# Linear attention and MLP on one core: batch 0's output products in half banks, copied and summed by ScalarE, and the sums over exponentials moved

## The chip, the core and the metric

The kernel runs on one core of a Trainium2 chip. The core has a matrix engine (TensorE, PE in the profile; PEld is its weight load), a vector engine (VectorE, DVE), an activation engine (ScalarE, ACT), GpSimd (POOL) and SyncE (SP). Each works through its own queue of instructions in order, and semaphores tie them together. DMAs are issued from the queues of SP, ACT and POOL. The metric is device time in microseconds (us); lower is better.

## The reference

q, k and v are 8 batches x 8 heads x 576 positions x 64, float32. Per head, with softmax over the 64 features for q and over the 576 positions for k:

```python
kv  = einsum('bhsd,bhse->bhde', softmax(k, axis=2), v)       # 64 x 64 per head
att = einsum('bhsd,bhde->bhse', softmax(q, axis=-1), kv)
x   = att.transpose(0, 2, 1, 3).reshape(8, 576, 512)
xn  = (x - mean(x)) / sqrt(var(x) + 1e-6) * g
out = x + relu(xn @ w1) @ w2                                 # w1 512 x 2048, w2 2048 x 512
```

## The kernel before

Of each batch the first 512 positions are handled as four tiles (t = 0 to 3) of 128 positions; the last 64 positions of all eight batches together form a ninth "batch", C9. (For batch 0 the k and v of all 576 positions are taken at once, two heads on 128 partitions.) The factor 1 / standard deviation is left out of xn and multiplied into the output at the end (`rstds`), so that the MLP need not wait for it.

All five engines are scheduled by hand: the order in which the program calls operations is the order in each engine's queue. `run` (L830) takes a list of main steps, the matmuls of one batch's MLP, each with a weight, and a list of side steps (position, function). A side step is called before the first main step that starts at or after its position. Positions are so a count of matmul work: one step of 512 columns weighs 1, one of 256 columns 0.5. Main steps of batch c carry the preparation of batch c + 1 and the loads and exponentials of batch c + 2 as side steps.

For batches from the third on (c = 2 to 8, `mm1_fast` L747 and `mm2_fast` L677), the products are made in blocks of 2 x 2 with seven products instead of eight, from sums of blocks that DVE and GpSimd make (`sum_w1` L221, `quarter_w2` L559, `sum_x` L236, `sum_h` L572). The first product takes positions 0 to 56, in two groups of 28: in each group ACT copies (L768, L772), then DVE adds into a bank (`add_5` L774, instruction L775), then product 7 runs in the bank that this add read, DVE writes hT (L778, L783) and PE goes on. The second product takes positions 56 to 112; at its end DVE writes quarters of the output (`y_quarter` L605, instruction L610), four pairs, which free the PSUM banks. DVE also makes the products x = po / sum (L421), centres them (L407) and sums the exponentials of q over features (`reduce_q` L208, L210); `recip_q` (L858) inverts the sums.

Batch 0 is special (`first_batch` L943). Its MLP starts as soon as its first tile is ready, and w1 arrives only then: the POOL queue issues, behind a small copy (`gate`, L995) that waits for the first half of q, the loads of v, the second half of q, w1 in five pieces (two of 256 columns, three of 512), w2, and then q, k and v of the next batches. PE does warming matmuls on zeros (`warm` L844) in between. exp(k) is spread by DVE (L282) and ACT (L278) into block-diagonal tiles of 128 x 128 (two heads each), cleared first by a memset (L988); the sums z and the products kv are then 36 full matmuls each (L289, L301). The output product po of a tile is one bank of 512 columns (L370). For tile 0 DVE makes mean and variance with bn_stats and bn_aggr (L384, L385), for tile 1 ACT sums the mean (L434); xn = (x - mean) * g, with g broadcast over partitions by a matmul of g's row (L1022). PE transposes xn, ACT copies the transposes out (`pe_T` L914).

The main steps of batch 0 are `mm1_part` (L499, weights 0 to 64; parts of four m, each 128 of the 2048 columns, times one or two tiles t) and `mm2_stream` (L548, 64 to 128). Beside them (L1103 to L1136) stand the rest of batch 0's tiles, the scaling of w1 by g (`scale_w1` L212, for later batches) and batch 1's preparation: exponentials of q (L193), `reduce_q`, transposes, `sum_w1`, the cast of v by DVE (`cast_v` L132, L134), the exponentials of k's last 64 positions (L179), `kv_mm` (L319, L333), `kv_out`, and then po, x, xn and the transposes of batch 1's tiles, before batch 1's first product at 128. The change goes through `first_batch`, this list, `prep_fast`, `attn_fast`, `second_side` and `attn_rest`.

Of the kernel before, what the change touches and what calls it, by code (L numbers as in the profile page):

```python
# [20 lines left out]
def kernel(  # L21
# [51 lines left out]
    gate = const.tile([P, 4], FP32)  # L73
# [4 lines left out]
    ones_f = const.tile([1, P], FP32)  # L78
    g_bc = const.tile([P, DM], FP32)
# [190 lines left out]
    def exp_k0(j):  # L270

        if j == 0:
            eks[0] = raw.tile([P, NP, T0, D], BF16, tag="kt", name="ek0", bufs=1)
        if j < NP - 1:
            nc.scalar.activation(eks[0][:, j], raws[0][0][:, j], AF.Exp)
            return
        for ps in halves:
            nc.scalar.activation(raws["ek"][ps, j, :, ps], raws[0][0][ps, j], AF.Exp)  # L278

    def spread_k0(j):  # L280
        for ps in halves:
            nc.vector.tensor_copy(out=raws["ek"][ps, j, :, ps], in_=eks[0][ps, j])  # L282

    def z0_mm(j):

        if j == 0:
            kvbox["z0"] = mm_ps.tile([P, DM], FP32, tag="m", name="z0")
        for t in range(T0):
            nc.tensor.matmul(  # L289
                kvbox["z0"][:, j : j + 1], raws["ek"][:, j, t], ones,  # L290
                start=(t == 0), stop=(t == T0 - 1),
            )

    def kv0_mm(j):

        if j != 1:
            pool, tag = (mm_ps, "m") if j == 3 else (att_ps, "a")
            kvbox["p0"] = pool.tile([P, 2, 256], FP32, tag=tag, name="pkv")
        pkv = kvbox["p0"]
        for t in range(T0):  # L300
            nc.tensor.matmul(  # L301
                pkv[:, j % 2, 0:D], raws["ek"][:, j, t], raws["v0"][:, j, t],
                start=(t == 0), stop=(t == T0 - 1),
            )
        if j:
            js = slice(0 if j == 1 else j, j + 1)
            rz = kvbox["rz"]
            for half, ps in enumerate(halves):
                if half and j > 1:
                    nc.scalar.activation(  # L310
                        kv_sb[ps, 0, j, ps], pkv[ps, j % 2, 0:D], AF.Copy, scale=rz[ps, j : j + 1]
                    )
                else:
                    nc.vector.tensor_mul(
                        kv_sb[ps, 0, js, ps], pkv[ps, slice(0, 2) if j == 1 else slice(j % 2, j % 2 + 1), 0:D],
                        rz[ps, js].to_broadcast([64, js.stop - js.start, D]),
                    )
# [64 lines left out]
    def stats(c, t, src, parts=(slice(0, 512),)):  # L382
        x, st, xn, mv = xs[c]
        nc.vector.bn_stats(st[:, t], src)  # L384
        nc.vector.bn_aggr(mv[:, t], st[:, t])  # L385
        for cols in parts:
            nc.vector.scalar_tensor_tensor(
                xn[:, t, cols], in0=src[:, cols], scalar=mv[:, t, 0:1], in1=g_bc[:, cols],
                op0=ALU.subtract, op1=ALU.mult,
            )  # L390

    def square_sum(c, t):
        x, _, _, mv = xs[c]
        if c:
            nc.scalar.activation(  # L395
                scrap, x[:, t], AF.Square, bias=mv[:, t, 0:1], scale=-float(DM),
                accum_out=mv[:, t, 1:2],
            )
        else:
            nc.scalar.activation(  # L400
                scrap, x[:, t], AF.Square, bias=mv[:, t, 0:1], accum_out=mv[:, t, 1:2]
            )

    def xn_out(c, t):
# [3 lines left out]
            out=xn[:, t], in0=x[:, t], scalar1=float(DM), scalar2=mv[:, t, 0:1],  # L408
            op0=ALU.mult, op1=ALU.subtract,
        )  # L410

    def xn_first(t):
        x, _, xn, mv = xs[0]
        nc.vector.scalar_tensor_tensor(
            xn[:, t], in0=x[:, t], scalar=mv[:, t, 0:1], in1=g_bc, op0=ALU.add, op1=ALU.mult
        )

    def x_fast(c, t):

        x, st, _, mv = xs[c]  # L420
# [4 lines left out]
            accum_out=mv[:, t, 0:1] if c else st[:, t, 0:1],  # L425
        )
        if c:
            xn_out(c, t)
        else:
            nc.vector.tensor_scalar_mul(out=mv[:, t, 0:1], in0=st[:, t, 0:1], scalar1=-1.0 / DM)  # L430
            xn_first(t)

    def mean_x(c, t):
        nc.scalar.activation(  # L434
            scrap, pobox[c, t], AF.Copy, scale=-1.0 / DM, accum_out=xs[c][3][:, t, 0:1]
        )

    def xn_sub(c, t):
        _, _, xn, mv = xs[c]
        nc.vector.scalar_tensor_tensor(  # L440
            xn[:, t], in0=pobox[c, t], scalar=mv[:, t, 0:1], in1=g_bc, op0=ALU.add, op1=ALU.mult
        )

    def square_po(c, t):
        mv = xs[c][3]
        nc.scalar.activation(
            scrap, pobox[c, t], AF.Square, bias=mv[:, t, 0:1], scale=1.0, accum_out=mv[:, t, 1:2]
        )

    def x_out(c, t):  # L450

        x = xs[c][0]
        if c == 1 or (c == 0 and t < 2):
            stats(c, t, pobox[c, t])
            return
        if c < B:
            nc.vector.tensor_mul(
# [730 lines left out]
```

## Time and profile before

| | us |
|---|---|
| median of three runs (268.95 to 269.48) | 269.26 |
| the profiled execution | 268.44 |
| its span, first to last instruction | 266.6 |
| PE busy | 259.1 (97%) |
| DVE busy | 220.2 (83%) |
| ACT busy | 178.6 (67%) |
| POOL busy | 90.6 (34%) |
| granted TensorE clock, mean | 0.999 |

The profiled execution is one more run; 1.8 us of its time lie outside the span. Times inside a view count from the start of the span. A timeline row gives start, duration, engine, source line, operation, what is written from what (buffer numbers left out) and the shape, how often, and in brackets the idle time before it with what ended it. In a DMA row the last number is the time from issue to landing.

### The profile page before, as it was taken

Reading aid. Unit: us, or ns where it says so; the run is one execution under the profiler, and the core shown is the slowest. Engines: PE = TensorE matmul, PEld = TensorE weight load, DVE = VectorE, ACT = ScalarE, POOL = GpSimd, SP = SyncE. Lnnn points to the kernel's source line nnn. Section 1 sums busy time; section 2 is a strip of 40 time slices with the busy share of each in tenths; the row PEclk is TensorE's granted clock in tenths of the full one; section 3 lists DMA queues with packets and bytes.
Section 4 is the critical chain, followed back from the end, with each engine's and each line's share of the span. In section 5 each row is a group of like instructions: output and inputs, shape, how many; then the busy total and the mean of one; then the engine's idle time right before and its main releaser. Section 6 shows DMA issues by size and latency. Waiting matters only on the chain. (4 is left out here: it accounts for less than half of the span.)

```text
span 266.6 us, 6696 instructions
## 1 busy us (share of the span) xinstructions
PE 259.1 (97%) x2634; PEld 218.4 (82%) x2634; DVE 220.2 (83%) x471; ACT 178.6 (67%) x349; POOL 90.6 (34%) x145
## 2 busy tenths in 40 slices
PE   8999999999999999999999999999999999999993
PEld 5778855775988998899889988998989788888882
DVE  7974995878999899789988988998799968877872
ACT  4767881796966886688668866786686378438400
POOL 6933126213069104930781088109100800030000
PEclk9999999999999999999999999999999999999999
DMA  6999999979966998899589948996935130422014
GB/s 216 220 203 207 325 223 303 278 171 279 176 131 195 303 111 133 246 288 117 92 265 267 127 87 278 257 138 126 261 60 101 42 119 4 79 81 79 2 39 118
DMA packets 82329, 45.00 MB, mean 169 GB/s; under 512 B 58037, under 2 KB 78521, under 8 KB 82298
## 3 DMA queue, kind: packets, MB, share of 16 engines
q0 software_dynamic: 32800, 22.29, 44.9%
q1 hardware_dynamic: 48906, 21.77, 37.6%
q10 hardware_dynamic: 592, 0.52, 0.6%
q8 instruction: 20, 0.33, 0.5%
q14 instruction: 11, 0.09, 0.1%
HBM read 36.70 MB, written 9.44 MB: 173 GB/s over the span
## 5 line engine op out<-in xcount | busy, mean ns | idle before, releaser
L599 PEld LDWEIGHTS <-hs 128*128 128x128 bf16 x512 | 49.5, 98 | 5.7
L744 PEld LDWEIGHTS <-w_q 128*128 128x128 bf16 x448 | 43.0, 98 | 6.8 <-issue 1.0
L248 POOL TENSOR_TENSOR tq<-xnT 128x256 bf16<-128x256 bf16 x24 | 15.6, 665 | 77.2 <-DMA xnT<-xn 63.9
L599 PEld LDWEIGHTS <-hT 128*128 128x128 bf16 x384 | 37.1, 98 | 4.4
L744 PEld LDWEIGHTS <-w1g 128*128 128x128 bf16 x336 | 32.2, 98 | 3.9
L599 PE MATMUL ba<-w_q,hs 128*128 128x256 bf16 x256 | 31.7, 273 | 0.0
L775 DVE TENSOR_TENSOR bb<-bx,s 128x512 f32<-128x512 f32 x28 | 18.3, 695 | 14.1 <-ACT s L772 14.0
L744 PE MATMUL bx<-tq,w_q 128*128 128x256 bf16 x224 | 29.2, 273 | 0.1
L768 ACT COPY bc<-bx 128x512 f32<-128x512 f32 x28 | 15.2, 594 | 16.8 <-PE bx L744 16.8
L421 DVE SCALAR_TENSOR_TENSOR x<-po,rq 128x512 bf16<-128x512 f32 x34 | 23.3, 686 | 2.2 <-PE po L370 2.0
L395 ACT ACTIVATE scrap<-x,mv 128x512 bf16<-128x512 bf16 x32 | 23.0, 720 | 1.7 <-DVE x L421 1.3
L616 POOL DMA_DIRECT2D out_dram<-ot x28 | 15.4, 558 | 24.1 <-DVE ot L610 24.0
L786 ACT ACTIVATE hT<-bc 128x512 bf16<-128x512 f32 x28 | 15.5, 598 | 11.7 <-PE bc L744 11.7
L583 DVE TENSOR_TENSOR hs<-hT 128x1024 bf16<-128x1024 bf16 x32 | 21.7, 685 | 1.3 <-ACT hT L786 1.2
L370 PE MATMUL po<-kv_sb,eqT 128*128 128x128 bf16 x128 | 21.2, 219 | 0.0
L210 DVE TENSOR_REDUCE zq<-eq 128x16 f32<-128x1024 bf16 (+1 forms) x20 | 20.6, 1048 | 0.5 <-ACT eq L193 0.5
L778 DVE TENSOR_TENSOR hT<-bx,s 128x512 bf16<-128x512 f32 x28 | 18.0, 686 | 3.2 <-PE bx L744 3.2
L786 ACT ACTIVATE hT<-bb 128x512 bf16<-128x512 f32 x28 | 15.3, 600 | 8.1 <-PE bb L744 8.1
L624 ACT COPY s<-ba 128x512 f32<-128x512 f32 x15 | 8.7, 579 | 13.4 <-PE ba L599 8.7
L599 PE MATMUL ba<-w_sb,hT 128*128 128x256 bf16 x128 | 16.7, 273 | 0.0
L599 PE MATMUL bb<-w_q,hs 128*128 128x256 bf16 x128 | 16.6, 273 | 0.0
L772 ACT COPY s<-bb 128x512 f32<-128x512 f32 x28 | 15.8, 620 | 0.7 <-PE bb L744 0.7
(152 smaller groups left out, 555.1 us busy)
## 6 DMA issues: line engine op xcount, KB each, us to landing
out_dram<-ot POOLq DMA_DIRECT2D x32, 256.0 KB, 6.2
qt<-in_q_dram SPq DMA_DIRECT2D x5, 1024.0 KB, 6.8
kt<-in_k_dram SPq DMA_DIRECT2D x5, 1024.0 KB, 13.4
w_sb<-in_moe_w_ch_dram POOLq DMA_DIRECT2D x4, 512.0 KB, 16.5
qt<-in_q_dram POOLq DMA_DIRECT2D x2, 1024.0 KB, 14.6
kt<-in_k_dram POOLq DMA_DIRECT2D x2, 1024.0 KB, 15.2
vm<-in_v_dram POOLq DMA_DIRECT2D x16, 128.0 KB, 13.0
w_raw<-in_moe_w_ch_dram POOLq DMA_DIRECT2D x3, 512.0 KB, 12.3
```

The costliest lines, as they stand in the source:

```text
L210: nc.vector.reduce_sum(eqs[c][1][:, ts], eqs[c][0][:, ts], axis=AX.X)
L248: eng.tensor_tensor(out=dst[:, t], in0=x[:, t], in1=y[:, t], op=ALU.subtract)
L370: nc.tensor.matmul(pobox["p"][:, i * P : i * P + P], eqTs[c][:, t, i, :], kv_sb[:, c, i, :], start=True, stop=True,)
L395: nc.scalar.activation(scrap, x[:, t], AF.Square, bias=mv[:, t, 0:1], scale=-float(DM), accum_out=mv[:, t, 1:2],)
L421: nc.vector.scalar_tensor_tensor(x[:, t].rearrange("p (h d) -> p h d", h=H), in0=pobox[c, t].rearrange("p (h d) -> p h d", h=H), scalar=1. ...
L583: nc.vector.tensor_tensor(out=dst, in0=x, in1=y, op=op)
L599: nc.tensor.matmul(hbox[bank][:, t], lhsT, rhs, start=first and (own or t == 0) and k == 0, stop=k == KH - 1, skip_group_check=True)
L744: nc.tensor.matmul(dst[:, q], lhsT, rhs, start=first and q == 0 and ko == 0, stop=ko == 1, skip_group_check=True)
L772: nc.scalar.copy(at[g, "s"], at[g, "b"])
L775: nc.vector.tensor_tensor(out=at[g, "b"], in0=at[g, "x"], in1=at[g, "s"], op=ALU.add)
L778: nc.vector.tensor_tensor(out=h_out(g, 1, 1), in0=at[g, "x"], in1=at[g, "s"], op=ALU.add)
L786: nc.scalar.activation(h_out(g, odd, half), at[g, name], AF.Relu)
```

## The change

- Batch 0: the block-diagonal tiles, their memset and the spreading copies go. z and kv are made by matmuls on 64 partitions and 64 output rows, two for each one before (144 instead of 72).
- The copy `gate` goes, so POOL issues v and all behind it without waiting for q. The broadcast of g and its row load go; g's columns are loaded from ACT's queue and made early.
- The output product of tiles 0 and 1 is made in two half banks; ACT copies each half to x and sums it in the same instruction; DVE adds the two sums and makes xn = 512 x - sum. The factor g / 512 comes in when DVE copies the transposes of batch 0's xn out of PSUM.
- Batch 0's first product goes in smaller parts at first (m 0 and 1, m 2 and 3 for each tile), and m 8 to 15 come last.
- Batch 1's preparation is placed 1 to 8.5 positions later, and three of the four second-half `sum_w1` move from batch 1 into batch 0, ahead of `cast_v`.
- The sums over the exponentials of q for batches 3 to 8 (C9 among them) move from the second product of one batch to positions 1 and 27 of the next one's first product; their reciprocal to 28. The exponentials of C9 move from 34-50 to 58-80, its transposes from 52 to 84.

```diff
@@ first_batch and its helpers
-        if j < NP - 1:
-            nc.scalar.activation(eks[0][:, j], raws[0][0][:, j], AF.Exp)
-            return
-        for ps in halves:
-            nc.scalar.activation(raws["ek"][ps, j, :, ps], raws[0][0][ps, j], AF.Exp)
+        nc.scalar.activation(eks[0][:, j], raws[0][0][:, j], AF.Exp)
...
         for t in range(T0):
-            nc.tensor.matmul(
-                kvbox["z0"][:, j : j + 1], raws["ek"][:, j, t], ones,
-                start=(t == 0), stop=(t == T0 - 1),
-            )
+            for ps in halves:
+                nc.tensor.matmul(
+                    kvbox["z0"][ps, j : j + 1], eks[0][ps, j, t], ones[ps],
+                    start=(t == 0), stop=(t == T0 - 1),
+                )
...
+    def po_half(t, half):
+
+        pool, tag = (mm_ps, "m") if half else (att_ps, "a")
+        po = pool.tile([P, DM], FP32, tag=tag, name="po")
+        for i in range(2):
+            j = 2 * half + i
+            nc.tensor.matmul(
+                po[:, i * P : i * P + P], eqTs[0][:, t, j, :], kv_sb[:, 0, j, :],
+                start=True, stop=True,
+            )
+        x, st, _, _ = xs[0]
+        nc.scalar.activation(
+            x[:, t, DH2 * half : DH2 * half + DH2], po[:, 0:DH2], AF.Copy,
+            accum_out=st[:, t, half : half + 1],
+        )
+
+    def sum_halves(t):
+        _, st, _, mv = xs[0]
+        nc.vector.tensor_add(mv[:, t, 0:1], st[:, t, 0:1], st[:, t, 1:2])
...
-        nc.gpsimd.tensor_copy(out=gate, in_=q0[:, 1, 0, 0:4])
...
@@ pe_T
+        elif g is None:
+            nc.vector.tensor_copy(out=dst[:, t], in_=ptr[:, :, 0:P])
         else:
-            nc.vector.tensor_copy(out=dst[:, t], in_=ptr[:, :, 0:P])
+            nc.vector.tensor_mul(dst[:, t], ptr[:, :, 0:P], g.to_broadcast([P, KO1, P]))
@@ mlp_steps
-            parts = ((0, 0, 1), (0, 1, 1), (1, 0, 2), (2, 0, 2), (0, 2, 2), (1, 2, 2), (2, 2, 2), (3, 0, 2), (3, 2, 2))
+            parts = ((0, 2, 0, 1), (0, 2, 1, 1), (2, 2, 0, 1), (2, 2, 1, 1), (4, 4, 0, 2), (0, 4, 2, 1),
+                     (0, 4, 3, 1), (4, 4, 2, 2), (8, 4, 0, 2), (8, 4, 2, 2), (12, 4, 0, 2), (12, 4, 2, 2))
@@ prep_fast, attn_fast, second_side, attn_rest
-        s += [(81, lambda: reduce_q(b, 0, 2)), (91, lambda: reduce_q(b, 2, 2))]
...
-        s = [(8, lambda: reduce_q(3, 2, 2))] if c == 3 else []
-        s += [(22 if c == 3 else 2, lambda: recip_q(c))]
+        s = [(1, lambda: reduce_q(c, 0, 2)), (27, lambda: reduce_q(c, 2, 2)), (28, lambda: recip_q(c))]
...
-        s += [(97, lambda: reduce_q(3, 0, 2))]
...
-        s += [(p, lambda i=i: sum_w1(i, 1)) for i, p in enumerate((30, 47, 58, 64))]
+        s += [(p, lambda i=i: sum_w1(i, 1)) for i, p in ((3, 30),)]
...
-        s = [(2, lambda: recip_q(C9)), (4, lambda: start_x(C9))]
-        for t, (p0, p1, p2) in enumerate(((14, 22, 46), (44, 54, 62), (58, 66, 69), (67, 75, 77))):
+        s = [(1, lambda: reduce_q(C9, 0, 2)), (27, lambda: reduce_q(C9, 2, 2)), (28, lambda: recip_q(C9)), (4, lambda: start_x(C9))]
+        for t, (p0, p1, p2) in enumerate(((14, 31, 46), (44, 54, 62), (58, 66, 69), (67, 75, 77))):
@@ the side steps of batch 0
-            + [(62, lambda: exp_q(1, 0, 4)), (64, lambda: exp_q(1, 2, 4))]
-            + [(67 + t, lambda t=t: reduce_q(1, t)) for t in range(T)]
+            + [(70, lambda: exp_q(1, 0, 4)), (72, lambda: exp_q(1, 2, 4))]
+            + [(75 + t, lambda t=t: reduce_q(1, t)) for t in range(T)]
...
-            + [(98.5 + 0.4 * j, lambda j=j: cast_v(1, j)) for j in range(2)]
             + [(p, lambda i=i: sum_w1(i, 0)) for i, p in enumerate((80, 84, 88, 92))]
-            + [(100.4, lambda: prep_kvrem(1))]
-            + [(100.5, lambda: kv_mm(1, range(T))), (102.0, lambda: (kv_mm(1, range(T, T + 1)), kv_out(1), start_x(1)))]
+            + [(p, lambda i=i: sum_w1(i, 1)) for i, p in enumerate((96, 98, 100))]
+            + [(103 + 0.4 * j, lambda j=j: cast_v(1, j)) for j in range(2)]
+            + [(104.5, lambda: prep_kvrem(1))]
+            + [(105, lambda: kv_mm(1, range(T))), (106, lambda: (kv_mm(1, range(T, T + 1)), kv_out(1), start_x(1)))]
@@ run B - 2
-                side += spread([lambda r=r: exp_qrem(r) for r in range(T)], 34, 50)
-                side += [(52, lambda: eq_T(C9))]
-                side += [(84 + 4 * t, lambda t=t: reduce_q(C9, t, 2)) for t in (0, 2)]
+                side += spread([lambda r=r: exp_qrem(r) for r in range(T)], 58, 80)
+                side += [(84, lambda: eq_T(C9))]
```

More of the change, by code (lines that the diff above doesn't have):

```diff
@@ L982, in first_batch @@
         nc.vector.memset(ones, 1.0)
-        nc.vector.memset(ones_f, 1.0)
         nc.vector.memset(bones, 0.0)
@@ L987, in first_batch @@
         nc.vector.memset(kv_sb, 0.0)
-        nc.vector.memset(ekp, 0.0)
         make_identity(nc, ident)
@@ L1118 @@
+                (22, lambda: square_sum(0, 0)),
+                (26, lambda: square_sum(0, 1)),
+                (30, lambda: square_sum(0, 2)),
+                (34, lambda: square_sum(0, 3)),
                 (38, lambda: rstd_op(0)),
             ]
-            + [(62, lambda: exp_q(1, 0, 4)), (64, lambda: exp_q(1, 2, 4))]
-            + [(67 + t, lambda t=t: reduce_q(1, t)) for t in range(T)]
-            + [((74, 78, 86, 90)[t], lambda t=t: eq_pT(1, t, nc.scalar)) for t in range(T)]
-            + [(78, lambda: nc.vector.reciprocal(eqs[1][2], eqs[1][1]))]
```

225 lines of the change are left out of this document (78 added, 147 removed).

## The prediction, made before the changed kernel ran

> **What bounds the kernel now.** I read the busy time by stretch first, to see where TensorE (PE) is not busy. Columns: stretch, its length, then busy us (instructions) of PE, PEld, DVE, ACT, POOL, the granted clock, the DMA share, GB/s.
>
> ```profile
> 0.00:16.00 16.00, 14.38 (x158) 10.93 (x159) 12.76 (x31) 9.49 (x17) 11.54 (x24) 1.00 0.95 215
> 16.00:20.00 4.00, 3.55 (x64) 3.17 (x61) 2.80 (x8) 2.66 (x6) 1.64 (x2) 1.00 1.26 206
> 81.00:184.00 103.00, 103.00 (x1106) 92.14 (x1104) 91.22 (x189) 77.04 (x149) 46.26 (x70) 1.00 1.08 193
> 185.00:212.00 27.00, 26.38 (x281) 23.20 (x280) 23.51 (x48) 17.99 (x39) 7.09 (x12) 1.00 0.48 113
> ...
> sum 238.00, PE 237.04 PEld 201.31 DVE 202.27 ACT 163.12 POOL 75.89; mean PE 33.86 PEld 28.76 DVE 28.90 ACT 23.30 POOL 10.84
> ```
>
> The sum row is over the stretches from 24 to 262 us. From 24 us on PE is a full queue: 237.04 of 238 us, and 103.00 of 103 in the middle. So the time is the moment at which the stream of matmuls starts, plus its work, plus holes of 0.96 us. The waits name them (total, times, longest):
>
> ```profile
> PE bb L744 <- DVE ot L610: 0.7, 2, 0.5
> PE bb L744 <- DVE kt L1079: 0.2, 1, 0.2
> ```
>
> They stand where one batch ends and the next begins: VectorE (DVE) is behind with the output quarters of L610, and a PSUM bank is not free. The start, in order of time (start, us, engine, instruction, idle before):
>
> ```profile
> 4.94 0.19 POOL L995 COPY gate<-qt 128x4 f32<-128x4 f32 x1 [1.68 <-DMA qt<-in_q_dram]
> 4.04 1.98 DVE L988 MEMSET v<- 128x2304 uint32 x1 [0.43 <-issue]
> 5.94 0.63 DVE L210 TENSOR_REDUCE zq<-eq 128x8 f32<-128x512 bf16 x1
> 8.28 1.38 ACT L278 ACTIVATE v<-kt 64x576 bf16<-64x576 f32 x2
> 7.45 2.78 DVE L282 COPY v<-ek 64x576 bf16<-64x576 bf16 x6
> 10.26 0.69 DVE L210 TENSOR_REDUCE zq<-eq 128x8 f32<-128x512 bf16 x1
> 7.89 3.02 POOL L96 DMA_DIRECT2D w_raw<-in_moe_w_ch_dram  x4
> w_raw<-in_moe_w_ch_dram POOLq DMA_DIRECT2D x1, 256.0 KB, 7.6
> w_raw<-in_moe_w_ch_dram POOLq DMA_DIRECT2D x1, 512.0 KB, 10.4
> 16.67 0.27 PE L507 MATMUL ph<-xnT,w_raw 128*128 128x128 bf16 x2 [0.39 <-ACT xnT L1048]
> 18.40 1.00 PE L507 MATMUL ph<-xnT,w_raw 128*128 128x128 bf16 x15
> 19.86 0.83 PE L507 MATMUL ph<-xnT,w_raw 128*128 128x256 bf16 x6
> 23.69 9.78 PE L507 MATMUL ph<-xnT,w_raw 128*128 128x256 bf16 x88
> 33.31 2.32 PE L552 MATMUL pc<-w_sb,hT 128*128 128x512 bf16 x10
> ```
>
> The stream starts at 16.67 us, waiting for ScalarE (ACT). The weights are hardly earlier: the four issues from 7.89 us on are 0.755 us apart, so w1's first piece lands at 7.89 + 7.6 = 15.5, and the third, issued at 9.4, at 9.4 + 10.4 = 19.8, where the 256-column matmuls of m 4 to 7 start (19.86). The first product of batch 0 ends at 33.31.
>
> **The change, part by part.** *Prologue.* DVE loses the memset L988 (which held the reduce until 5.94, about 0.4 us after the exponential), six spreading copies (2.78, between the two normalisations, 7.45 to 10.26) and the statistics. The first normalisation runs from 5.94 to 7.45, where the copies begin, 1.5 us; so the second moves from 10.26 to about 7.0, right behind it. ACT takes its four half copies of the products, each about 0.55 by half of the 0.60 row below plus its 0.19:
>
> ```profile
> 15.15 0.60 ACT L434 ACTIVATE scrap<-po 128x512 bf16<-128x512 f32 x1
> 15.64 0.19 ACT L434 ACTIVATION_READ_ACCUMULATOR scrap<-po 128x1 f32 x1
> 10.18 0.74 PEld L289 LDWEIGHTS <-v 128*128 128x128 bf16 x27 [0.76 <-issue]
> 42.28 0.70 PE L333 MATMUL pkv<-vm,ek 128*64 128x65 bf16 x32
> ```
>
> The sums z and the products kv go from 72 full matmuls to 144 on quarters of the array, a shape that the trace lacks. Nearest rows: a full one paces at 0.027 us (0.74 over 27), one of 128 x 64 at 0.016 ((0.70 - 0.20) / 31). Bounds: 144 x 0.008 (pairs side by side) to 144 x 0.027, 1.2 to 3.9, against 2.0 now; I take 0.016, 2.3 us, the nearest row. The Trainium skill ("TensorEngine Tiling (Array Packing)", Instruction Overhead) gives each matmul some 60 cycles whatever its size, which speaks against 72 more of them; at the full clock my estimate from it is 25 ns each, 1.3 us later in the chain. The 16 ns row disagrees.
>
> The chain is then, by estimate from these rows: ACT ends k's exponentials at 9.66 now (8.28 + 1.38); one of them (0.69) goes, as the last is no longer done by halves, and a copy of 0.60 comes before them, so 9.6, or 9.9 with k a little later (next part). The last quarter of z, three fillers and kv (72 x 0.016) take 1.8, to 11.7; two scalings of 0.3, to 12.3; two half copies on ACT, to 13.4; sum, centring, transposes and product with g at about 0.3 each, to 14.6, or 15.4 with the dear bound. w1's first piece is as late, so the stream starts at 15.1 to 15.4, some 1.4 earlier. DVE takes three products with g from ACT (0.7 each); DVE is busy 2.80 of 4 there, and behind that cover w1's third piece sets the pace. g's columns now come by ACT's queue, idle until q lands, and g's row leaves SP's; I count neither. Of the sums of squares ACT does one operation less than now, beside PE.
>
> *The gate.* Without L995 the v loads are issued 1.7 us earlier, and the POOL queue behind them. What that brings depends on whether DMA was idle, which no view shows directly: DMA share 0.95 over the first 16 us against 1.26 after. Bounds for the queue's shift s: 0 (the same engines, only another order, and k later) to the whole 1.68 of the wait. I take 0.4, as the share says mostly full. The Trainium skill ("DMA: Bandwidth & Descriptors", the part on queues, rings and completion order) has each engine take turns between its queues, so that an earlier v buys its time from k: by it s is near 0 and k0's last piece is later.
>
> *The stream.* With 19.4 for the third piece: 96 matmuls of 256 columns at 0.109 (9.78 over 88, less the last one's tail) 10.5, 32 of 128 at 0.056 (1.00 over 15, likewise) 1.8, a set of transposes 0.2, holes 0.3: the first product ends at 32.2, 1.1 earlier than 33.31. The finer split (32 narrow for 16 wide) costs 1.79 - 1.75, nothing.
>
> *But what is late next?* Batch 1's preparation hangs on a DVE chain that does not move with PE:
>
> ```profile
> 33.13 1.99 ACT L193 ACTIVATE eq<-qt 128x1024 bf16<-128x1024 f32 x2
> 35.16 2.47 DVE L210 TENSOR_REDUCE zq<-eq 128x8 f32<-128x512 bf16 x4 [0.50 <-ACT eq L193]
> 37.92 0.69 DVE L234 TENSOR_TENSOR w_q<-w1g 128x512 bf16<-128x512 bf16 x2
> 39.88 0.75 DVE L234 TENSOR_TENSOR w_q<-w1g 128x512 bf16<-128x512 bf16 x2
> 41.23 0.77 DVE L134 COPY vm<-vt 128x1024 bf16<-128x1024 bf16 x2 [0.61 <-DMA vt<-in_v_dram]
> 50.67 1.91 PE L507 MATMUL ph<-xnT,w1g 128*128 128x256 bf16 x16
> qt<-in_q_dram POOLq DMA_DIRECT2D x1, 1024.0 KB, 18.3
> 14.76 0.90 POOL L118 DMA_DIRECT2D qt<-in_q_dram  x1 [1.33 <-DMA qt<-in_q_dram]
> ```
>
> q of batch 1 lands at 14.76 + 18.3 = 33.06, the exponentials run to 35.12, the sums to 37.6, then four sum_w1 at 0.655 (37.92 to 39.88 is three), then cast_v. The change puts three more sum_w1 (2.0 us) before cast_v: 37.92 + 7 x 0.655 + 0.77 = 43.3, less s = 42.9. PE comes to kv_mm(1) four steps of 0.216 (2.32 over 10, less the tail) later than now: 42.28 - 1.1 + 0.86 = 42.0, so it stands still about 0.9 us, in order, with the rest of batch 0's second product behind it. From there to batch 1's first product it is 50.67 - 42.28 - 0.86 = 7.5: 50.5 instead of 50.67. **Of the 1.1 us only 0.2 is left.** The cap also makes this part insensitive: a stream up to 0.9 us later changes nothing.
>
> *Moved sums.* Each reduce of two tiles leaves the second product for positions 1 and 27 of the next batch's first product:
>
> ```profile
> 105.52 0.88 DVE L610 SCALAR_TENSOR_TENSOR ot<-ba,rstd,x 128x256 f32<-128x256 f32 x2
> 107.75 1.30 DVE L775 TENSOR_TENSOR bb<-bx,s 128x512 f32<-128x512 f32 x2 [1.08 <-ACT s L772]
> 111.63 0.43 DVE L783 TENSOR_SCALAR hT<-hT 128x1024 bf16<-128x1024 bf16 x1
> 113.02 0.69 DVE L583 TENSOR_TENSOR hs<-hs,hT 128x1024 bf16<-128x1024 bf16 x1
> 114.76 1.30 DVE L775 TENSOR_TENSOR bb<-bx,s 128x512 f32<-128x512 f32 x2 [1.04 <-ACT s L772]
> 115.78 1.04 PE L744 MATMUL bx<-tq,w_q 128*128 128x256 bf16 x8
> 207.17 1.21 DVE L210 TENSOR_REDUCE zq<-eq 128x16 f32<-128x1024 bf16 x1
> ```
>
> The first fits: 106.40 + 1.21 = 107.6, before L775 at 107.75; the two load-triggering memsets behind it, and so SP's loads of q and k, go 1.2 us later, with over 10 us to spare. The second fits just: 112.06 + 1.21 + 0.26 for the reciprocal + 1.3 for two sum_h = 114.8, against 114.76; PE needs the result at 115.78, with 0.1 to 0.3 to spare. Cost 0. In return DVE has 2.4 us less before the quarters of L610, more than the longest hole needs, so I count all 0.96 as gone. C9's exponentials and SP's transposes move 24 to 32 places later, and the transposes are still 42 places (about 9 us) ahead of their use; hidden.
>
> Sum: -0.2 - 0.96 = -1.15 on the profiled execution's 268.44 (span 266.6), 267.3. The median of the three runs shown is 269.26; taking the same step off it gives **268.1**.
>
> **Rivals.**
> *Whole gain.* The POOL queue moves up by most of 1.68. Then the chain from q moves up as far as ACT, busy with batch 0's last outputs, lets it, by about 1.0: cast_v ends at 42.3, batch 1's first product starts at 49.9, -0.8 - 0.96, 267.5. For it: 1.68 us of POOL waiting is real; against it: the DMA share. By the Trainium skill's rule of turns, named above, this would not come at all. Chance 0.17.
> *The sums free nothing.* DVE comes to the end of a batch as late as now because the work only came earlier in the same queue, so the 0.96 stays and only 0.2 is won: 269.1, no change that could be told (a measurement of this kernel tells about 0.2%, 0.5 us). For it: DVE is busy 91.22 of 103. Against it: the hole before L775 takes one sum whole. Chance 0.15.
> *The sums stand before the add.* At position 27 the reduce delays L775, and PE stops before product 7, in each of six batches (from the third on, all but the last, which has no batch behind it). Price p a batch: between 0 and 1.5, all of a reduce and the reciprocal. At p = 0.19 the gain is gone, from p = 0.28 it is slower by over 0.2%; with 0.35, 268.1 + 2.1 = 270.2. For it: my margin is 0.1. Chance 0.20.
>
> **How the numbers follow.** Forecast 0.48, between 267.6 and 268.7. Faster by over 0.2%: 0.48 + 0.17 = 0.65; within: 0.15; slower: 0.20. The range goes from 267.0 (the whole gain, should q's chain move by 1.5 instead of 1.0) to 270.0 (the last rival at p = 0.32); it leaves out the dearer part of that rival, about 0.12, and some 0.05 below.
>
> **What would show it.** First batch-0 product at 15.1 to 15.4 (the line numbers are those of before); L552 starting near 32.2; PE waiting some 0.9 us for DVE's vm (L134) ahead of L333 near 42 us; batch 1's first L507 near 50.5; no wait of L744 on L610. I am wrong if PE has no hole near 42 (whole gain), or has one before product 7 in every batch.

## The result, and the profile after

| | before | after |
|---|---|---|
| median of four runs each, us | 269.12 (268.95 to 269.48) | 266.51 (266.17 to 266.79) |
| the profiled execution | 268.44 | 266.63 |
| its span | 266.6 | 264.8 |
| PE / DVE / ACT busy | 259.1 / 220.2 / 178.6 | 257.6 / 217.0 / 175.1 |

The ratio is 0.9897, 95% interval 0.9884 to 0.9909: faster by 1.0%, where 268.1 (0.4%) was forecast. The medians differ by 2.6 us, the two profiled executions by 1.8 us; both differences have to be explained, the second first.

The same stretches as in the prediction, now of the changed kernel (stretch, length, then busy us of PE, PEld, DVE, ACT, POOL, granted clock, DMA share, GB/s):

```profile
81.00:184.00 103.00, 102.78 (x1064) 91.45 (x1065) 90.11 (x188) 76.66 (x149) 46.87 (x72) 1.00 1.15 194
185.00:212.00 27.00, 26.83 (x286) 23.66 (x285) 24.27 (x49) 18.22 (x39) 8.39 (x15) 1.00 0.47 117
```

PE was busy 103.00 of 103 between 81 and 184 us before; now it is 102.78. Toward 212 us it is the other way round, 26.38 before and 26.83 now. So the holes have not gone, they have moved. The prologue and batch 0, in order of time (the timeline of the changed kernel: start, duration, engine, line; the lines are those of the changed kernel):

```profile
5.78 3.03 POOL L93 DMA_DIRECT2D w_raw<-in_moe_w_ch_dram  x4
10.64 1.30 PE L296 MATMUL pkv<-v,ek 64*64 64x64 bf16 x72
12.90 0.90 POOL L115 DMA_DIRECT2D qt<-in_q_dram  x1 [1.00 <-DMA qt<-in_q_dram]
14.96 0.70 PE L456 MATMUL ph<-xnT,w_raw 128*128 128x128 bf16 x8 [0.31 <-DMA w_raw<-in_moe_w_ch_dram]
18.78 1.91 PE L456 MATMUL ph<-xnT,w_raw 128*128 128x256 bf16 x16
31.49 2.00 ACT L190 ACTIVATE eq<-qt 128x1024 bf16<-128x1024 f32 x2
31.53 1.67 PE L501 MATMUL pc<-w_sb,hT 128*128 128x512 bf16 x6
33.66 2.46 DVE L207 TENSOR_REDUCE zq<-eq 128x8 f32<-128x512 bf16 x4
40.92 0.76 DVE L131 COPY vm<-vt 128x1024 bf16<-128x1024 bf16 x2
41.50 0.88 PE L321 MATMUL pkv<-vm,ek 128*64 128x65 bf16 x32
49.34 1.91 PE L456 MATMUL ph<-xnT,w1g 128*128 128x256 bf16 x16
```

The POOL queue issues w1 at 5.78 instead of 7.89; its first piece lands at 14.9 instead of 15.5. The stream of batch 0 starts at 14.96 instead of 16.67, and now waits for w1, no longer for ACT. Batch 0's second product starts at 31.53 (33.31 before), and batch 1's first product at 49.34 instead of 50.67: 1.33 us earlier, where 0.2 were forecast. (That place moves a little from one execution to the next: in e5, the same kernel again, it is 49.62.)

From there on I follow the batches by the start of the first group of `bx<-xnT,w1g`, which opens each batch from the third to the ninth. Differences between successive starts, in us; 26.21 is the least that any batch took in these two traces:

| batch (starting in before) | 3rd (78.77) | 4th | 5th | 6th | 7th | 8th (210.44 to 237.69) | sum |
|---|---|---|---|---|---|---|---|
| before | 26.54 | 26.21 | 26.21 | 26.21 | 26.50 | 27.25 | 158.92 |
| after | 26.22 | 26.40 | 26.41 | 26.70 | 26.21 | 26.68 | 158.62 |

Three holes of before have gone or shrunk (0.32, 0.29 and 0.57), and three batches lose time that they did not lose before (0.19, 0.20, 0.49). Net 0.30 us are gained, of the 0.96 forecast. With 1.33 at batch 1 and 0.17 behind the last matmuls this makes the 1.8 us of the traces.

### The profile page after: what moved, and what is told of

It reads as the page before. It is cut to its first block, busy times and chain, and to the rows that moved or that the text cites. A ratio compares the mean times of both kernels' runs of the same rounds, so it can differ in the third digit from the quotient of the medians.

```text
span 264.8 us, 6827 instructions
## 1 busy us (share of the span) xinstructions
PE 257.6 (97%) x2708; PEld 217.5 (82%) x2711; DVE 217.0 (82%) x465; ACT 175.1 (66%) x346; POOL 90.4 (34%) x144
## 5 line engine op out<-in xcount | busy, mean ns | idle before, releaser
L372 ACT ACTIVATE scrap<-x,mv 128x512 bf16<-128x512 bf16 x36 | 25.9, 719 | 1.7 <-DVE x L388 1.3
L565 POOL DMA_DIRECT2D out_dram<-ot x28 | 15.4, 556 | 24.1 <-DVE ot L559 24.0
L207 DVE TENSOR_REDUCE zq<-eq 128x16 f32<-128x1024 bf16 (+1 forms) x20 | 20.6, 1049 | 2.0 <-ACT eq L198 2.0
L724 DVE TENSOR_TENSOR bb<-bx,s 128x512 f32<-128x512 f32 x28 | 18.2, 694 | 4.1 <-ACT s L721 4.0
L358 PE MATMUL po<-kv_sb,eqT 128*128 128x128 bf16 x120 | 20.5, 219 | 0.0
L501 PE MATMUL pc<-w_sb,hT 128*128 128x512 bf16 x61 | 15.8, 379 | 0.2
```

What stands on the lines that cost most here:

```text
L207: nc.vector.reduce_sum(eqs[c][1][:, ts], eqs[c][0][:, ts], axis=AX.X)
L358: nc.tensor.matmul(pobox["p"][:, i * P : i * P + P], eqTs[c][:, t, i, :], kv_sb[:, c, i, :], start=True, stop=True,)
L372: nc.scalar.activation(scrap, x[:, t], AF.Square, bias=mv[:, t, 0:1], scale=-float(DM), accum_out=mv[:, t, 1:2],)
L501: nc.tensor.matmul(hbox["pc", t], hbox["h"][:, ko, t, :], w2_sb[:, ko, :], start=(ko == 0), stop=(ko == KO2 - 1),)
L724: nc.vector.tensor_tensor(out=at[g, "b"], in0=at[g, "x"], in1=at[g, "s"], op=ALU.add)
```

## The experiments

What had to be told apart: whether the earlier stream comes from the POOL queue or from the shorter chain; which edit closed the holes of before, and which opened the new ones; and why the medians differ by 0.8 us more than the traces. My first theory was that the whole queue shift had arrived and that the moved sums had closed the old holes; the rivals are named with each run. Every ratio is to the kernel before on the same chip, whose median there was 269.0 to 269.2 us. The granted clock in what follows is the mean TensorE clock that each run lists.

### The copy `gate` put back, and taken out of before

```diff
 # e1: the changed kernel              # e2: the kernel before
+ nc.gpsimd.tensor_copy(out=gate,      - nc.gpsimd.tensor_copy(out=gate,
+     in_=q0[:, 1, 0, 0:4])            -     in_=q0[:, 1, 0, 0:4])
```

e1: 

> The changed kernel with the small POOL copy that waits for the first half of q put back ahead of the loads of v. Queue theory (DMA was not full between 5 and 12 us, so without the copy the whole POOL queue moves up by its wait, and w1 and batch 1's q with it): first product of batch 0 near 15.5 us instead of 14.96, its first product stage ending near 32.6 instead of 31.53, q of batch 1 landing near 33 instead of 31.5, batch 1's first product near 50.6 instead of 49.34, and the kernel 1.0 to 1.4 us slower than the changed one, about 267.7. Chain theory (the shorter compute chain before the first product is what counts, the loads are early enough either way): batch 1's first product within 0.3 us of 49.34, and the kernel within 0.4 us of the changed one, about 266.7.

e2: 

> The kernel before with only that POOL copy taken out. Queue theory: loads land 1.6 us earlier here too, but the old compute chain still starts the stream at about 16.3 us (0.4 earlier, as the second half of q is there sooner), so only part comes through: 0.3 to 0.8 us faster than before, about 268.5. If the queue alone made the gain, with no need of the shorter chain: 1.3 us or more faster, below 267.9. Chain theory: within 0.2 us of before.

e1 took 268.00 us (266.53 to 269.18, 12 runs), ratio 0.9954 (0.9937 to 0.9971); e2 269.06 us (267.82 to 270.75, 12 runs), ratio 0.9991 (0.9971 to 1.001). The granted clock enters both. Six of the twelve runs of e1 have a clock of 0.994 or less, which none of ten runs of the changed kernel has; the other six have a median of 267.4 us, against 266.33 for those ten. So the wait for q costs some 1.1 us in the changed kernel at a like clock, and half of the runs lose clock with it. Of e2, four runs have a clock of 1.00 and take 267.82 to 267.87 us, 0.5 less than the runs of before at a full clock (268.34); the other eight have 269.2, as before has in most of its runs (269.21). So of the 0.3 to 0.8 us expected of e2, 0.5 are there at a full clock, and nothing in the median. Two rows of e1's timeline, then one of e2's:

```profile
4.95 0.19 POOL L935 COPY gate<-qt 128x4 f32<-128x4 f32 x1 [1.69 <-DMA qt<-in_q_dram]
17.02 0.62 PE L457 MATMUL ph<-xnT,w_raw 128*128 128x128 bf16 x8 [2.21 <-DMA w_raw<-in_moe_w_ch_dram]
```

```profile
16.13 0.27 PE L506 MATMUL ph<-xnT,w_raw 128*128 128x128 bf16 x2
```

The two edits need each other. With the queue moved up alone (e2) the stream starts at 16.13 instead of 16.67, as the old chain through DVE and ACT still stands in front of it (PE's transposes of xn come at 15.38 in both traces); with the shorter chain alone (e1) PE waits 2.21 us for w1 and starts at 17.02; with both it starts at 14.96. (In e1 the first piece of w1 takes 9.1 us to land, in before 7.6 from the same time of issue; why is open.)

### The moved sums put back, and moved alone

```diff
 # e3 (and e9, the same kernel again): the changed kernel, sums of batches 3 to 8 at their old places
+ s += [(81, lambda: reduce_q(b, 0, 2)), (91, lambda: reduce_q(b, 2, 2))]
- s = [(1, lambda: reduce_q(c, 0, 2)), (27, lambda: reduce_q(c, 2, 2)), (28, lambda: recip_q(c))]
+ s += [(22 if c == 3 else 2, lambda: recip_q(c))]
 # (likewise (97 / 8) for batch 3 and 84 + 4 * t for C9)
 # e4: the kernel before with these sums moved, and C9's exponentials, transposes and first centring moved with them
 # e6: the changed kernel, only the sums of position 27 (and the reciprocals) back
 # e5: the changed kernel as it is
```

e3: 

> The changed kernel with the sums over the exponentials of batches 3 to 8 and C9 at their old places in the second products (the exponentials and transposes of C9 stay at their new places). Theory of the holes (the sums held up the output quarters, and PE for a bank): the holes of about 0.9 us at the batch boundaries come back, and the kernel is 0.4 to 0.9 us slower than the changed one, about 267.1. Rival (the sums free nothing, they stand in the same queue earlier): within 0.2 us of the changed one.

e4: 

> The kernel before with only the sums over the exponentials, their reciprocals and C9's exponentials and transposes moved as in the change. Theory of the holes: 0.4 to 0.9 us faster than before, about 268.4, with PE's holes after 24 us at most 0.5 us in all. Rival (they free nothing): within 0.2 us of before. Rival (the sum at position 27 delays the add before product 7): slower than before by 0.5 us or more, with a hole of PE before product 7 in each batch.

e5: 

> The changed kernel as it is, to have its time on the same chip as the next three kernels. Both theories: 266.2 to 266.8 us, the granted clock at 0.997 or above in nearly all runs.

e6: 

> The changed kernel with only the second half of the moved sums (position 27, and the reciprocal behind it) back in the second product; the first half stays at position 1. Theory A (position 27 alone delays the add that product 7 waits for): about as good as with both halves back, 265.4 to 265.9, and the first groups of the batches follow each other by 26.21. Rival B (either half costs by DVE's load): half of the gain, 266.0 to 266.2, and some batches still take 26.4. Rival C (the moved sums free DVE at the end of the batch, the earlier run was faster by its prologue): no faster than the changed kernel.

e9: 

> The changed kernel with all moved sums back in the second products, once more, to have its time on the same chip as the next three. Expected 265.4 to 266.0, the batches 26.21 apart.

Measured: e3 265.68 us (0.9876, 0.9857 to 0.9896), e9 265.62 (0.9876, 0.9853 to 0.9899), e5 266.24 (0.9896, 0.9877 to 0.9915), e6 266.50 (0.9908, 0.9888 to 0.9929), e4 268.24 (0.9969, 0.9957 to 0.9982). My expectation for e3 was wrong in sign: the changed kernel is faster without the moved sums (ten runs of e3 and e9 have a median of 265.64, ten of the changed kernel 266.33). In e9 the batches follow each other by 26.21, five times, and 26.29: of the holes of before only 0.08 in the eighth batch is left, though the sums are where they were before. So the moved sums did not close them. In e6 four batches take 26.21, but the third 26.58 and the eighth 26.66; its median is no better than the changed kernel's, so theory A (position 27 alone) falls too. Rival C has that number right, but not its reason: e9 repeats the gain of e3. e4 gains 0.9 us on before with the same prologue; its batches take 26.42, 26.44, 26.50, 26.34, 26.21 and 26.65, so the hole of the seventh batch closes there too, that of the eighth in part (27.25 before), and others open. The sum of these times is only 0.36 us below that of before; the rest of e4's gain its trace does not show. That two things were moved together in e4 is what the next runs take apart.

### The loads ahead of the sum

```diff
 # e12: the changed kernel
- side += [(1, lambda b=c + 2: load_batch(b))]
+ side += [(0.9, lambda b=c + 2: load_batch(b))]
```

> The changed kernel with the loads of the batch after the next at position 0.9, so that the memsets that release them stand ahead of the first moved sum on VectorE, not behind it. Theory (the sum ahead of them makes the loads of q and k 1.2 us later, they run into the transposes of xn, and GpSimd's sums and product 5 come late): the loads are issued 1.1 us after a batch begins as in e9, and the 0.49 us lost near 157 us go: 265.6 to 266.1, while the 0.4 near 210 us stay. Rival (the late transposes come from elsewhere): that period keeps 26.7 and the time stays at 266.2 to 266.6.

266.13 us (266.02 to 266.29), ratio 0.9887 (0.9871 to 0.9904). In time this cannot be told from the changed kernel (0.9896, 0.9877 to 0.9915); the traces can be compared. In e12 five batches take 26.21, all but the eighth (26.71). First the changed kernel's timeline, then e12's:

```profile
131.06 1.21 DVE L207 TENSOR_REDUCE zq<-eq 128x16 f32<-128x1024 bf16 x1
132.21 0.06 DVE L1022 MEMSET qt<- 1x1 f32 x1
132.32 0.39 SPq L115 DMA_DIRECT2D qt<-in_q_dram  x1
156.11 1.30 POOL L245 TENSOR_TENSOR tq<-xnT 128x256 bf16<-128x256 bf16 x2 [15.09 <-DMA xnT<-xn]
157.46 1.03 PE L693 MATMUL bb<-tq,w_q 128*128 128x256 bf16 x8
158.71 1.03 PE L693 MATMUL bx<-tq,w_q 128*128 128x256 bf16 x8 [0.22 <-ACT s L721]
```

```profile
131.11 0.06 DVE L1022 MEMSET qt<- 1x1 f32 x1
131.22 0.39 SPq L115 DMA_DIRECT2D qt<-in_q_dram  x1
154.44 1.30 POOL L245 TENSOR_TENSOR tq<-xnT 128x256 bf16<-128x256 bf16 x2 [12.42 <-DMA xnT<-xn]
157.18 1.04 PE L693 MATMUL bb<-tq,w_q 128*128 128x256 bf16 x8
```

In the changed kernel the sum at position 1 (L207) stands ahead of the memset that releases the loads. The load of q is issued 1.1 us later; 24 us on, GpSimd waits for the transpose of xn until 156.11, makes its sums late, and product 5 (`bb<-tq`), which reads them, takes 1.25 us to the next product instead of 0.87. With the loads first the transposes are there at 154.44. That a late load collides with the transposes on the DMA engines was my reading, and that the order of two instructions on DVE decides it. The trace of e6, which keeps the sum at position 1, speaks against the second:

```profile
132.59 0.39 SPq L115 DMA_DIRECT2D qt<-in_q_dram  x1
154.26 1.30 POOL L245 TENSOR_TENSOR tq<-xnT 128x256 bf16<-128x256 bf16 x2 [12.95 <-DMA xnT<-xn]
```

There the load is issued as late, yet the transpose is there at 154.26, and the batch takes 26.21. e1, with the same order, has no loss in this batch either; e5, the changed kernel again, has it (26.76). So the late load is at most one of several things that must come together for these 0.5 us, and what the others are stays open.

The loss of 0.19 and 0.20 in the fourth and fifth batch sits before product 7 of the second group, where the third rival had it. The changed kernel (timeline), then e12:

```profile
109.98 0.75 DVE L732 TENSOR_SCALAR hT<-hT 128x1024 bf16<-128x1024 bf16 x1
113.42 1.29 DVE L724 TENSOR_TENSOR bb<-bx,s 128x512 f32<-128x512 f32 x2
114.17 1.20 PE L693 MATMUL bx<-tq,w_q 128*128 128x256 bf16 x8
136.38 0.74 DVE L732 TENSOR_SCALAR hT<-hT 128x1024 bf16<-128x1024 bf16 x1
163.28 0.43 DVE L732 TENSOR_SCALAR hT<-hT 128x1024 bf16<-128x1024 bf16 x1
```

```profile
110.20 0.46 DVE L732 TENSOR_SCALAR hT<-hT 128x1024 bf16<-128x1024 bf16 x1
114.35 1.04 PE L693 MATMUL bx<-tq,w_q 128*128 128x256 bf16 x8
```

The chain of the prediction is there, add (L724) behind the reduce of position 27, and it does fit as long as L732 takes 0.43 us. In exactly the two batches in which L732 took 0.74 or 0.75 the margin of 0.1 to 0.3 us was used up and product 7 took 0.16 longer; in e5's trace it is one batch (0.75 at 84.03) and one loss of 0.19. In before and in e9, where no sum stands behind it, an L732 (L783 in before) of 0.73 or 0.74 us costs nothing: those batches take 26.21. What stretches L732 was not tried.

### The eighth batch, and the third

```diff
 # e11: e9 with C9's exponentials, transposes and first centring at their places of before
- side += spread([lambda r=r: exp_qrem(r) for r in range(T)], 58, 80); side += [(84, lambda: eq_T(C9))]
+ side += spread([lambda r=r: exp_qrem(r) for r in range(T)], 34, 50); side += [(52, lambda: eq_T(C9))]
 # (and x_fast of tile 0 at 22 for 31)
 # e10: e9 with the three sum_w1 at their places of before, in batch 1's stage
- + [(p, lambda i=i: sum_w1(i, 1)) for i, p in enumerate((96, 98, 100))]
+ s += [(p, lambda i=i: sum_w1(i, 1)) for i, p in enumerate((30, 47, 58, 64))]
```

e11: 

> The changed kernel with all moved sums back and the remainder's exponentials, transposes and first centring at their old positions (34 to 50, 52 and 22). Theory (their move 24 to 32 places later closed the holes of 0.30 at 194 us and 1.0 at 210 to 212 us): the last two periods are 26.5 and 27.2 again, 266.6 to 267.1. Rival (these holes went with the prologue's shift): 265.4 to 266.0.

e10: 

> The changed kernel with all moved sums back and the three sums over w1 back in batch 1's stage. Theory (these three, taken out of batch 1's second half, are what closed the hole of 0.34 us at 80 us, and they cost 0.2 ahead of kv_mm(1)): batch 1's first product 0.2 earlier, the period from batch 2 to batch 3 is 26.5 again instead of 26.21, in sum 0.1 to 0.2 slower than e9. Rival (the hole at 80 was closed by the earlier start alone): the period stays 26.21, 0.2 faster than e9.

e11 took 266.69 us (266.29 to 267.11), ratio 0.9907 (0.9892 to 0.9923): 1.1 us more than e9. Its batches take 26.22, 26.20, 26.22 and 26.20, then 26.50 and 27.02, nearly as in before. Its timeline has the same holes:

```profile
209.04 1.04 PE L693 MATMUL bx<-xnT,w1g 128*128 128x256 bf16 x8
210.34 0.61 PE L693 MATMUL bb<-tq,w_q 128*128 128x256 bf16 x4 [0.26 <-DVE ot L559]
```

So the later place of C9's exponentials and transposes (with the first centring, which moved along) closed the hole of 0.29 and most of that of 1.04; 0.29 and 0.73 of them come back here. I had put these holes down to the moved sums and costed C9's move at nothing. What the changed kernel keeps of the second hole (26.68 against e9's 26.29) has its place on DVE. The changed kernel, then e9:

```profile
206.00 2.65 POOL L245 TENSOR_TENSOR tq<-xnT 128x256 bf16<-128x256 bf16 x4 [18.58 <-DMA xnT<-xn]
206.69 1.42 DVE L245 TENSOR_TENSOR tq<-xnT,tq 128x256 bf16<-128x256 bf16 x2 [1.48 <-POOL tq L245]
```

```profile
205.47 2.90 POOL L245 TENSOR_TENSOR tq<-xnT 128x256 bf16<-128x256 bf16 x4 [18.95 <-DMA xnT<-xn]
206.73 0.48 DVE L245 TENSOR_TENSOR tq<-xnT,tq 128x256 bf16<-128x256 bf16 x2
```

With the sums gone from there, DVE stands ready and waits 1.48 us for GpSimd's first result, then takes 1.42 us for two subtractions beside GpSimd's own; in e9 a reduce fills the wait and the two take 0.48, while GpSimd's four take 2.90 instead of 2.65. The last output quarters (`ot<-ba`, L559) then start 0.83 us behind the new batch's first group (210.21 against 209.38) instead of 0.43 (209.30 against 208.87 in e9): the 0.4 that the batch loses. The Trainium skill ("SBUF — State Buffer", two separate sides) says that a DVE operation with two inputs in SBUF and a GpSimd operation that reads SBUF hold one port pair in turn, each for its whole instruction. Here the two DVE instructions took some 0.7 us each, as long as one of GpSimd's four, and 0.24 in e9, where GpSimd's four took 0.25 longer: this agrees.

e10 took 265.53 us (265.42 to 265.78), ratio 0.9866 (0.9849 to 0.9883): the same as e9. Its timeline shows why:

```profile
41.41 0.70 PE L321 MATMUL pkv<-vm,ek 128*64 128x65 bf16 x32
78.06 0.60 PE L693 MATMUL bb<-tq,w_q 128*128 128x256 bf16 x4
78.83 0.38 PE L693 MATMUL bb<-tq,w_q 128*128 128x256 bf16 x2 [0.17 <-DVE kt L1025]
```

Without the three sums ahead of it, kv_mm(1) runs in 0.70 us instead of 0.88, and batch 1's first product starts at 49.08 (49.34 to 49.72 in the seven traces that have the changed prologue without the gate and the three sums ahead, 49.72 in e9). But the third batch takes 26.54 again: the hole of before at 80 us is back (0.33). The theory was right on both effects, the 0.33 and the earlier kv_mm(1), but had the second too small: they about cancel. In both traces DVE has no gap worth naming in the 12 us before the third batch, so I read it as the bound there; where three of its sums stand then decides only at which place PE waits.

### The clock

Both profiled executions ran at a full clock. The runs without a view still give their mean granted clock, and there the kernels differ. Of 74 runs of before beside these experiments, 58 have a clock of 0.9945 or less and a median of 269.21 us; seven have 0.9985 or more, and a median of 268.34; the nine between have 269.09, so that the mean clock does not fix the time of each run. All ten runs of the changed kernel have 0.996 or more. So 0.87 us go with the clock in before, about the 0.8 us by which the medians moved more than the traces. The profiled execution of before, on which the prediction's sum was made, was of the rarer kind.

```diff
 # e7: before                                # e13: before
+ warm(2)  # ahead of kv0_mm(0)              + warm(3)  # behind z0_mm(0)
+ warm(4)  # behind kv0_mm(1)                + warm(2)  # ahead of each later z0_mm
                                             + warm(4)  # behind kv0_mm(1)
 # e8: the changed kernel                    # e14: the changed kernel
- warm(5), warm(3)  # between the z0_mm      - warm(5), warm(3)  # between the z0_mm
- warm(2), warm(3), warm(7), warm(2)  # behind kv
```

e7: 

> The kernel before with two filler matmuls before kv0_mm(0) and four before the transposes of tile 1, where PE stands idle between 10 and 12 us. Clock theory (the stretch at half clock comes after PE stood idle there, and costs about 0.8 us in most runs of before): most runs at a granted clock of 0.997 or above, median 268.0 to 268.6, while before stays near 269.2. Rival (the clock's fall is chance, or set by something other than PE's idle time): the same share of runs below 0.995 as before, median 269.2 to 269.5.

e8: 

> The changed kernel without its 22 filler matmuls behind the first transposes. Clock theory: many runs fall to 0.987 to 0.994, a stretch of some 3.3 us at 0.50 shows in the profile between 11 and 21 us, and the median is 0.6 to 1.1 above that of the changed kernel. Rival: the clock stays above 0.997 and the time within 0.3 of the changed kernel's, or below it, as PE no longer works on fillers ahead of the chain.

e13: 

> The kernel before with nine fillers between the steps of z (three, then two ahead of each of the other three) and four between the products kv of pairs 0 and 1 and the transposes of tile 1. Clock theory (the half clock comes from the thin stretch of one-column matmuls from 8 to 11 us): the granted clock is 0.998 or above in most runs, and since the fillers also make the chain up to 0.8 us longer, the median is 268.2 to 269.0. Rival (the stretch is set by something else): most runs stay at 0.990 to 0.995 and the median is 269.2 to 270.0.

e14: 

> The changed kernel without the eight fillers between the steps of z; the fourteen behind the products kv stay. Clock theory (the stretch around z counts): runs fall below 0.995 as in before, and the median is 0.4 to 0.9 above the changed kernel's. Rival (only the stretch behind kv counts, where the fourteen fillers stay): the clock stays at 0.997 or above and the time within 0.3 of the changed kernel's 266.2 to 266.5.

e8 took 267.09 us (0.9931, 0.9907 to 0.9954), 0.85 more than e5 on the same chip, and all six runs fell to 0.984 to 0.992. e14 took 266.86 us (before had 269.04 there; 0.9914, 0.9892 to 0.9937), and four of its six runs are at 0.994 or less. So the fillers around z count. Whether those behind kv count besides, six runs of six against four of six cannot tell. And fillers are not all: e1 has every one of them and fell in six of twelve runs, so that taking out the copy `gate` keeps the clock up too. In the rows below, the granted clock is the figure behind the busy times. First e14, then e13:

```profile
7.00:9.80 2.80, 2.37 (x67) 1.75 (x64) 2.26 (x6) 1.92 (x4) 1.82 (x3) 1.00 1.19 223
9.80:16.70 6.90, 6.66 (x115) 5.74 (x116) 2.25 (x9) 2.90 (x11) 4.27 (x6) 0.51 1.28 233
16.70:19.00 2.30, 1.83 (x28) 1.39 (x27) 1.57 (x5) 0.80 (x2) 0.90 (x2) 1.00 1.24 207
```

```profile
8.30:11.70 3.40, 3.29 (x55) 2.24 (x56) 3.21 (x8) 2.44 (x4) 3.22 (x5) 1.00 1.06 186
11.70:15.10 3.40, 3.40 (x45) 2.98 (x42) 1.32 (x6) 1.03 (x3) 2.23 (x4) 0.50 1.22 212
15.10:18.00 2.90, 2.73 (x31) 2.12 (x29) 2.00 (x5) 2.27 (x6) 1.60 (x3) 1.00 1.30 207
```

The clock falls to a half and stays there for about 6.9 us in e14 and for 3.4 us in e13, and in e13 PE counts as busy throughout: 3.40 of 3.40 us, with fewer matmuls. The busy time does not show it. The Trainium skill ("TensorE: Matmul & The Clock Gate", Part 1) tells of a monitor that sets the rate by the activity in windows of 3.4 us which run freely, whenever a kernel starts; stretches of one and two times 3.4 us agree, and the free run fits a kernel that sometimes falls and sometimes not.

In before, fillers did not settle it. e7 took 268.99 us (0.9995, 0.9976 to 1.0014), with 7 of 12 runs above 0.9945 and no gain in the median; e13 269.81 us (1.0011, 0.9993 to 1.0028), with 5 of 12; before itself has 16 of 74 above 0.9945. In e13's row the window ahead of the fall was 97% busy, fillers included, and the clock fell all the same. So that the fillers of the changed kernel keep the clock up is shown by taking them out (e8, e14); which of before's instructions lets it fall stays open. The stretch holds the 1 x 512 float32 matmul of g's broadcast, which the change takes out; that was not tried by itself.

## Why the prediction missed

**The gate.** The step "I take 0.4, as the share says mostly full" is the largest miss on the trace. q of batch 1 is issued at 12.90, 1.86 us earlier, and lands 18.6 us later, at 31.5, against 33.06: the shift s was 1.56 there, nearly the whole 1.68. For the first piece of w1, where the prediction used the same s, it was only 0.6 (14.9 against 15.5), though that piece is issued 2.11 us earlier. The DMA rows of the changed kernel, then two of before:

```profile
kt<-in_k_dram SPq DMA_DIRECT2D x4, 288.0 KB, 4.7
w_raw<-in_moe_w_ch_dram POOLq DMA_DIRECT2D x2, 256.0 KB, 9.2
w_raw<-in_moe_w_ch_dram POOLq DMA_DIRECT2D x1, 512.0 KB, 13.7
qt<-in_q_dram POOLq DMA_DIRECT2D x1, 1024.0 KB, 18.6
```

```profile
kt<-in_k_dram SPq DMA_DIRECT2D x4, 288.0 KB, 4.7
w_raw<-in_moe_w_ch_dram POOLq DMA_DIRECT2D x2, 256.0 KB, 8.2
```

q takes about as long from issue to landing as before (18.3) and only starts earlier. v loses a part of its shift on the way: it takes 6.4 us instead of 5.8, and 6.8 in e2. The first two pieces of w1 take 1.0 longer; they do in e1 too, where they are issued as late as in before, so this is not the price of the earlier issue alone. k's pieces, which by the prediction's rule of turns would pay for an earlier v, take 4.7 in both. That the engines had room shows in the stretch from 8 to 12 us, of before and then of after:

```profile
8.00:12.00 4.00, 3.61 (x69) 2.65 (x67) 3.81 (x9) 2.72 (x5) 3.79 (x6) 1.00 1.01 187
12.00:20.00 8.00, 7.38 (x114) 6.37 (x115) 5.67 (x16) 5.24 (x12) 3.90 (x5) 1.00 1.28 213
```

```profile
8.00:12.00 4.00, 4.00 (x158) 3.34 (x156) 1.96 (x7) 1.42 (x3) 3.03 (x5) 1.00 1.17 257
```

In after the stretch carries 257 GB/s instead of 187, and in e2, where only the gate is gone, 260. The share does not tell this. In before it is 1.01 at 187 GB/s here, 1.28 at 213 right behind, and 1.05 at 352 from 3 to 7 us: a higher share is not more data. I had read the 0.95 of the first 16 us as "mostly full" without asking what the engines moved. The rule of turns, by which s would be near 0, did not decide for q of batch 1; v did lose time on the way, as sharing would have it. The rival "whole gain" was right on the queue.

**The chain in front of the stream** held: 144 quarter matmuls at 0.016 (72 of them in 1.30 us, less a tail of 0.19, make 0.0156 each), first product forecast at 15.1 to 15.4, measured 14.96, with w1 as the bound on the other side. The 25 ns of my estimate from the Trainium skill's "TensorEngine Tiling (Array Packing)" (Instruction Overhead) did not hold here.

**What is late next** held in form, and only s was off. With s = 1.56 the prediction's own sum for the end of cast_v, 43.3 - s, gives 41.7; the row says 40.92 + 0.76 = 41.68. PE came to kv_mm(1) at about the forecast distance and lost 0.2 instead of 0.9 us. ACT was not the cap that the rival "whole gain" had put at 1.0: its exponentials start at 31.49, as soon as q is there.

**The holes.** "I count all 0.96 as gone", because DVE has 2.4 us less before the quarters, failed in its cause and in its size: 0.30 net were gained. The old holes go by C9's move (e11) and the earlier stage of the three sums (e10), which I costed at nothing or for another effect; the moved sums open new ones of 1.3 us together (0.19 + 0.20 + 0.49 + 0.39, against e9), which "cost 0" in the prediction. So the rival "the sums free nothing" was right about the sums, but the holes went by other edits. The step "the loads go 1.2 us later, with over 10 us to spare" counted the spare time only to the loads' own reader; whether the 0.49 come from there stays open (e12 against e6). The rival "the sums stand before the add" was right in mechanism, at 0.2 us in two batches of six instead of in all.

**The median.** "The same step taken off" the median of 269.26 fails, as the change also keeps the clock up, a term that the sum put at nothing and that one execution at full clock could not show. With the 1.8 us of the traces alone the median would have come to 267.5; the 0.8 that go with the clock bring it to 266.5, below the 267.0 to which the prediction's range went. Sum of the steps against the traces: -1.15 forecast; -1.13 more at batch 1, +0.66 less at the holes, -0.17 at the end, together -1.8; and -0.8 by the clock.

**The best version** of those run is the changed kernel with the sums left in the second products (e3, e9; e10 is level with it): 265.6 us, ratio 0.9876, against 0.9896 for the changed kernel (e5, on the chip of e3).

## What to carry to other kernels

Whether DMA engines are full cannot be read from their busy share alone: look at the GB/s beside it, and at what the same engines move elsewhere in the same trace. What an earlier issue is worth differs from one transfer to the next: here 2.11 us at the issue became 0.6 at the landing of w1's first piece, and 1.86 became 1.56 for q of batch 1. When an instruction is moved in an in-order queue, ask of everything behind it which transfers it releases, and of these not only when their reader needs them but what else is on the DMA engines when they arrive. Two things that come late in one trace are not yet cause and effect: find a run that has the first without the second. And compare the granted clock of all runs with that of the profiled one before a sum made on the trace is carried over to the median.

## What the runs showed of the hardware

- PE busy and PE at half speed look alike: 3.40 of 3.40 us busy at a granted clock of 0.50 (e13). Runs of before that lose clock take about 0.9 us more (269.21 against 268.34).
- Two subtractions of 128 x 256 bf16 on DVE took 1.42 us beside GpSimd's and 0.48 in another order, with GpSimd's 2.90 instead of 2.65.
- Sixteen DMA engines at a share of 1.01 still took in 70 GB/s more (187 to 257) when their issues came earlier. In the trace of before, a share of 1.05 goes with 352 GB/s and one of 1.28 with 213.
